# Blocks of 256 queries, values at the end of a pass in a shared bank, and a part of the exponentials on VectorE, in a two-layer transformer on one core

## The chip, the core and the metric

The kernel runs on one core of one Trainium2 chip. A core has TensorE (PE) for matrix products, ScalarE (ACT), VectorE (DVE), GpSimd (POOL) and SyncE (SP), which issues the DMAs here. Each has its own list of instructions, and semaphores make one engine wait for another. PSUM is the memory that TensorE writes to here; the kernel uses eight banks of it, each 512 float32 columns on 128 partitions. The metric is the device time of the whole kernel in microseconds (us).

## The reference

Two layers with the same weights, each an attention and an FFN on x of 2048 x 448 (bfloat16), 16 heads of 28 columns, FFN width 1792:

```python
def _A_ref(x, wqkv, wo):                     # H = 16, Dh = 28
    qkv = (x @ wqkv).reshape(B, S, 3, H, Dh).transpose(2, 0, 3, 1, 4)
    q, k, v = qkv[0], qkv[1], qkv[2]
    p = softmax(einsum("bhqd,bhkd->bhqk", q, k) * Dh ** -0.5)
    o = einsum("bhqk,bhkd->bhqd", p, v)
    return o.transpose(0, 2, 1, 3).reshape(B, S, D) @ wo
def _B_ref(x, w1, b1, w2, b2):
    r = maximum(x @ w1 + b1, 0)
    return (r * r) @ w2 + b2
x = A_x
for _ in range(2):
    x = x + _A_ref(layernorm(x), A_wqkv, A_wo)
    x = x + _B_ref(layernorm(x), B_w1, B_b1, B_w2, B_b2)
```

The softmax needs 16 x 2048 x 2048 exponentials per layer, 134 million in all.

## The kernel before, in words

**A planner orders the work.** The kernel is Python that emits instructions. `Planner.run` holds some generators ("streams"), each with a priority. Each yields one `Op` at a time: the engine, an estimated duration, what it depends on (`deps`), a buffer that it acquires (`acq`, a `Res`) and buffers that it gives back (`rel`). The planner always takes the op that can start first on its own clock, ties by priority, and emits its instructions there. So the order on each engine is fixed when the kernel is built, and the chip only follows it with semaphores. A product of TensorE that would make the scores late is put off (`SLACK`).

**Attention.** Queries are taken in blocks (`blocks`, L164): in layer 0 four of 512 rows, in layer 1 two of 512, two of 256, four of 128. Heads go in four groups `g` of four heads, each head padded to 32 partitions, so that four heads' small products lie beside one another in TensorE's array. A *pass* is one query block, one `g` and a range of key tiles. It is cut into *units* of 512 score columns: one head and one 128-key tile for 512 queries, or two key tiles for 256, four for 128. Three units make a *group*: 2048 units, 683 groups.
- `s_stream` (priority 0, L543): scores of a group, keys as rows and queries as columns, into `sc`, three PSUM banks, two such buffers (`R_sc`).
- `e_stream` (priority 1, L558): one exponential on ScalarE, 128 x 1536 from `sc` to `pt` in SBUF (bfloat16), with the softmax's scale.
- `p_stream` (priority 2, L593): values. As soon as the four heads of a step have their exponentials, four products add into the bank `oT`, which belongs to it alone (`ps_o`). A ones column beside V's 28 columns gives the softmax's sums. At the end of a pass VectorE copies `oT` out (L617), or adds it to an earlier part (L619).
- `norm_stream` (priority 3): three small DMAs on SP spread the sums over partitions, to DRAM and back as a broadcast (L650, L662, L669), with VectorE's reciprocal between (L656), then a product (L679). The last block of a layer does it without DMAs (L635, L641).

**The rest of a layer.** When a block's four groups of heads are normalised, `chain` (priority 4 and on) does the output projection (`wo`, L690 adds to x), layernorm (`bn_stats` L310, a Newton rsqrt of 12 small VectorE instructions L331 to L340, L384), transposes (L359, L369), FFN (L417; ReLU L719 on VectorE, or L717 on ScalarE where no scores are left; square L726), and in layer 0 layernorm and QKV of layer 1 for its rows. `mm_tile` (L399) is the helper of all these products: it has one PSUM bank (`ps_m`, `R_m`), and its VectorE evacuation must be planned before the generator goes on. `first_block` does layernorm and QKV of layer 0, 512 rows at a time.

**Layer boundary.** Layer 1 needs all its keys. Its first passes are cut: block 0 with key tiles 0 to 11, block 1 with the same for two groups of heads (`AHEAD`), then tiles 12 to 15 of these.

**Filler.** `heat` (L763) adds products without use where TensorE's planned load over 2.8 us is under 0.74.

PSUM: six banks for the two `sc`, one for `oT`, one for `mm_tile`.

Of the kernel before, what the change touches and what calls it, by code (L numbers as in the profile page):

```python
# [13 lines left out]
P = 128  # L14
# [4 lines left out]
QB = 512  # L19
EPS = 1e-5  # L20
MAGIC = 0x5F3759DF
WARM = 34
GATE = [None, ('Q', 0, 0, 0), ('Q', 0, 1, 0), ('Q', 0, 3, 0)]
AHEAD = range(2)
SLACK = 0.6
WINDOW = 2.8

# [13 lines left out]
class Op:  # L41
    __slots__ = ("eng", "dur", "fn", "deps", "acq", "rel", "mode", "sets", "start", "end", "res", "turn", "ready", "lat", "need", "got")

    def __init__(self, eng, dur, fn, deps=(), acq=None, rel=None, mode="full", sets=(), lat=0.0, need=1):
        self.eng = eng if isinstance(eng, tuple) else (eng,)
        self.dur, self.fn, self.deps, self.mode, self.lat = dur, fn, deps, mode, lat
        self.rel = rel if isinstance(rel, list) else ([] if rel is None else [rel])
        self.acq = acq if isinstance(acq, tuple) else (() if acq is None else (acq,))
        self.sets = sets if isinstance(sets, list) else ([sets] if sets else [])
        self.start = self.end = self.res = self.turn = None  # L50
        self.need, self.got = need, []
# [5 lines left out]
class Planner:  # L57
# [3 lines left out]
    def __init__(self):  # L61
        self.clock = {"PE": 0.0, "ACT": 0.0, "DVE": 0.0, "POOL": 0.0, "DMA": 0.0, "-": 0.0}
        self.mode = None
        self.tok = {}
        self.streams = []
        self.past = []

    def load(self, span):

        now = self.clock["PE"]  # L70
        return sum(e - max(s, now - span) for s, e in self.past if e > now - span) / span
# [5 lines left out]
    def earliest(self, o):  # L77
        t = 0.0
        for d in o.deps:
            if not isinstance(d, Op):  # L80
                d = self.tok.get(d)
            if d is None or d.end is None:
# [3 lines left out]
                                (0.0 if same and d.eng[0] != "DMA" else LAT[d.eng[0]])))  # L86
        if o.acq:
            free = [r.when() for r in o.acq if r.when() is not None]
# [13 lines left out]
    def run(self):  # L102
        while self.streams:
# [16 lines left out]
            if o.acq:  # L120
                o.res = min((r for r in o.acq if r.when() is not None), key=lambda r: r.when())
# [4 lines left out]
            if e == "PE":  # L126
                self.mode = o.mode
                self.past = [p for p in self.past if p[1] > s - 8.0] + [(s, o.end)]
# [13 lines left out]
def kernel(  # L142
# [19 lines left out]
    scale = float(DH) ** -0.5  # L162

    blocks = [[(0, 4), (4, 4), (8, 4), (12, 4)], [(0, 4), (4, 4), (8, 2), (10, 2), (12, 1), (13, 1), (14, 1), (15, 1)]]  # L164
# [5 lines left out]
    ptp = ctx.enter_context(tc.tile_pool(name="ptp", bufs=4))  # L170
    xtp = ctx.enter_context(tc.tile_pool(name="xtp", bufs=3))
    hp = ctx.enter_context(tc.tile_pool(name="hp", bufs=NFC))
    rp = ctx.enter_context(tc.tile_pool(name="rp", bufs=2))
    np_ = ctx.enter_context(tc.tile_pool(name="np_", bufs=2))
    sp = ctx.enter_context(tc.tile_pool(name="sp", bufs=4))
    dp = ctx.enter_context(tc.tile_pool(name="dp", bufs=2, space=bass.MemoryType.DRAM))
    ps_sc = ctx.enter_context(tc.tile_pool(name="ps_sc", bufs=2, space=bass.MemoryType.PSUM))
    ps_o = ctx.enter_context(tc.tile_pool(name="ps_o", bufs=1, space=bass.MemoryType.PSUM))
    ps_m = ctx.enter_context(tc.tile_pool(name="ps_m", bufs=1, space=bass.MemoryType.PSUM))
# [3 lines left out]
    R_sc, R_o, R_m, R_pt = Res(2), Res(1), Res(1), Res(4)  # L183
    R_xt, R_os, R_xn, R_h, R_on, R_rec = Res(3), Res(2), Res(2), Res(1), Res(2), Res(2)
# [16 lines left out]
    part_sb = const.tile([P, G, QB], DT.float32, name="part_sb")  # L201


    k0_f32 = K_sb[0][:, :, :].rearrange("p g s -> p (g s)").bitcast(DT.float32)
    part = [[part_sb[:, g, :] for g in range(G)], [k0_f32[:, g * QB:(g + 1) * QB] for g in range(G)]]
    st_qk = part_sb[:, :, :].rearrange("p g q -> p (g q)").bitcast(DT.bfloat16)[:, 0:NDC * 2 * D]
# [8 lines left out]
    def setup():  # L215
# [15 lines left out]
        idle = ps_o.tile([P, QB], DT.float32, name="oT")  # L231
# [57 lines left out]
    def bank(o, name):  # L289

        if o.res is R_m:
            return ps_m.tile([P, 512], DT.float32, name=name, tag="m")[:, :]
# [3 lines left out]
    def pools_now(early=False):  # L296
        return (R_m, R_sc) if early or len(s_left) == 0 else (R_m,)

    def engs_now(early=False):
        return ("ACT", "DVE") if (early and ("s", 0) not in pl.tok) or len(s_left) == 0 else ("DVE",)  # L300
# [3 lines left out]
    def moments():  # L304
        return sp.tile([P, 4, 2], DT.float32, name="mv"), []

    def stats(mv, t0, j, deps):
        def fn(e):
            st = sp.tile([P, 6], DT.float32, name="st")
            nc.vector.bn_stats(out=st[:, :], in_=x_sb[:, t0 + j, :])  # L310
# [5 lines left out]
    def layernorm(t0, nt, deps_of, early=False, mv=None):  # L316
# [7 lines left out]
        mv = mv[0]  # L324
        rstd = sp.tile([P, 4], DT.float32, name="rstd")

        def rsqrt(e):
            ve = sp.tile([P, 4], DT.float32, name="ve")
            tt = sp.tile([P, 4], DT.float32, name="tt")
            y, v, t = rstd[:, 0:nt], ve[:, 0:nt], tt[:, 0:nt]  # L330
            nc.vector.tensor_scalar(out=v, in0=mv[:, 0:nt, 1], scalar1=EPS, scalar2=None, op0=ALU.add)  # L331
            yi = y.bitcast(DT.int32)
            nc.vector.tensor_scalar(out=yi, in0=v.bitcast(DT.int32), scalar1=1, scalar2=None,
                                    op0=ALU.arith_shift_right)
            nc.vector.tensor_scalar(out=yi, in0=yi, scalar1=-1.0, scalar2=float(MAGIC),
                                    op0=ALU.mult, op1=ALU.add)
            for _ in range(3):
                nc.vector.scalar_tensor_tensor(out=t, in0=y, scalar=-0.5, in1=y, op0=ALU.mult, op1=ALU.mult)
                nc.vector.tensor_tensor(out=t, in0=t, in1=v, op=ALU.mult)
                nc.vector.scalar_tensor_tensor(out=y, in0=t, scalar=1.5, in1=y, op0=ALU.add, op1=ALU.mult)  # L340
        rs = Op("DVE", 2.3, rsqrt, deps=[last])
# [3 lines left out]
        def take(e):  # L345
            box["x"] = xtp.tile([P, NDC, QB], DT.bfloat16, name="xnT")
# [28 lines left out]
        for p0 in range(0, nt, 2):  # L375
# [4 lines left out]
            for j in js:  # L380
                xn = xns[2 * (own.turn % 2) + j % 2]

                def norm(e, j=j, xn=xn):
                    nc.vector.tensor_scalar(out=xn[:, 0:D], in0=x_sb[:, t0 + j, :],  # L384
                                            scalar1=mv[:, j, 0:1], scalar2=rstd[:, j:j + 1],
# [13 lines left out]
    def mm_tile(subs, evac, ev_dur, deps, any_engine=False, sets=(), early=False):  # L399
# [7 lines left out]
        while i < len(mms):  # L407
# [5 lines left out]
            def fn(e, part=mms[i:k], i=i):  # L413
                if i == 0:
                    box["t"] = bank(first, "mt")
                for c0, n, lhsT, rhs, a, b in part:
                    nc.tensor.matmul(box["t"][:, c0:c0 + n], lhsT=lhsT, rhs=rhs, start=a, stop=b)  # L417
            last = Op("PE", dur, fn, deps=list(deps) if i == 0 else [last],
                      acq=pools_now(early) if i == 0 else None)
# [3 lines left out]
        e = Op(engs_now(early) if any_engine else ("DVE",), ev_dur, lambda e: evac(e, box["t"]), deps=[last], rel=first, sets=sets)  # L423
        yield e
        return e

    def copy_to(dst):
        def f(e, t):
            src = t[:, :] if len(dst.shape) == 2 else t[:, :].rearrange("p (r n) -> p r n", r=dst.shape[1])
            if e == "ACT":  # L430
# [5 lines left out]
    def qkv(l, t0, nt, xnT, own_xt, ends, early=False):  # L436
# [4 lines left out]
        def turned(w, dst, key, wkey, g0):  # L441
# [5 lines left out]
                copy_to(d), 0.70, [*ends, *[(wkey, g) for g in range(g0, g0 + r)]], True,  # L447
# [42 lines left out]
    def first_block(blk):  # L490
        early = blk == 0
        xnT, own_xt, ends = yield from layernorm(4 * blk, 4, lambda j: [("x", blk, j // 2)] + ([] if early else [GATE[blk]]), early)
        yield from qkv(0, 4 * blk, 4, xnT, own_xt, ends, early)
# [9 lines left out]
    add_passes(0, [0], [0, 4, 8, 12, 16])  # L503
    for qb in range(1, len(blocks[0])):
        add_passes(0, [qb], [0, 16])
    add_passes(1, [0], [0, 12])
    add_passes(1, [1], [0, 12], AHEAD)
    add_passes(1, [0], [12, 16])
    add_passes(1, [1], [12, 16], AHEAD)
    add_passes(1, [1], [0, 16], range(AHEAD[-1] + 1, G))  # L510
    for qb in range(2, len(blocks[1])):
        add_passes(1, [qb], [0, 16])
# [8 lines left out]

    def s_stream():
        for gi, us in enumerate(groups):
            deps = set()
            mm = 0
            for pi, kb, r, hh in us:
# [6 lines left out]
            def fn(e, gi=gi, us=us):  # L533
                sc = gbuf[gi]["sc"] = ps_sc.tile([P, 3 * 512], DT.float32, name="sc", tag="sc")
                for i in range(4):
                    for k, (pi, kb, r, hh) in enumerate(us):
                        if i >= r:
# [10 lines left out]
                                   sets=("s", gi))  # L548
# [3 lines left out]
    def e_stream():  # L552
        for gi, us in enumerate(groups):
            n = len(us) * 512

            def fn(e, gi=gi, n=n):
                pt = gbuf[gi]["pt"] = ptp.tile([P, 3 * 512], DT.bfloat16, name="pt")
                nc.scalar.activation(out=pt[:, 0:n], in_=gbuf[gi]["sc"][:, 0:n], func=AF.Exp, scale=scale)  # L558
            o = gbuf[gi]["e"] = Op("ACT", n / 1200 + 0.068, fn, deps=[("s", gi)], acq=R_pt,
                                   rel=gbuf[gi]["s"], sets=("e", gi))  # L560
            yield o

# [3 lines left out]
    def p_stream():  # L566


        where = {}
        for gi, us in enumerate(groups):  # L570
            for k, (pi, kb, r, hh) in enumerate(us):
                where.setdefault((pi, kb), []).append((gi, k, hh))
        steps = list(where.items())
        last_use = {}
        for si, (_, parts) in enumerate(steps):
            for gi, _, _ in parts:
                last_use[gi] = si
        for si, ((pi, kb), parts) in enumerate(steps):
            l, qb, g, kbs, first, last = passes[pi]
            r = 4 // blocks[l][qb][1]  # L580
            n = blocks[l][qb][1] * P
            opens = kb == kbs[0]
            closes = kb + r - 1 == kbs[-1]
            if opens:
                box = {}

            def fn(e, kb=kb, parts=parts, box=box, opens=opens, l=l, g=g, kbs=kbs, r=r, n=n):
                if opens:
                    box["t"] = ps_o.tile([P, QB], DT.float32, name="oT")
                for i in range(r):  # L590
                    for gi, k, hh in parts:
                        c0 = k * 512 + i * n
                        nc.tensor.matmul(box["t"][DHP * hh:DHP * hh + DHP, 0:n],  # L593
                                         lhsT=V_sb[l][:, kb + i, 4 * g + hh, :],
# [214 lines left out]
```

The softmax here doesn't subtract the row's maximum and nothing guards it: scores larger than these inputs give would overflow.

## Time and profile before

| | |
|---|---|
| median of 4 runs | 964.77 us (963.82 to 967.0) |
| the profiled execution | 964.71 us |
| its span, first to last instruction | 962.9 us |
| mean granted TensorE clock | 0.991 |
| ScalarE busy | 929.5 us |
| TensorE busy, weight loads | 855.0 us, 326.2 us |
| VectorE busy | 433.6 us |

The span is what the profile covers; the execution's own time is 1.8 us longer. A line of the groups reads: line of the kernel, engine, operation, out <- in by the program's names, shape, count; after the first bar the busy microseconds and the mean nanoseconds of one; after the second the idle time of the engine just before them and whom it waited for. Busy time counts overlapping instructions once. Means hold their own overlap, so that busy time over count is the price of one in a full engine. In the slices a digit is tenths of a fortieth of the span.

Some lines of the page for orientation: the TensorE clock in the slices, and the DMA queues.

```profile
PEclk9899999999999999999999999999999999999999
...
q1 hardware_dynamic: 24556, 16.02, 5.8%
```

### The profile page before, as it was taken

How to read it: one execution, taken by the hardware profiler on the slowest of the kernel's cores; microseconds unless marked ns; L12 is line 12 of the kernel's file. 1: busy time of each engine (PE TensorE's matmuls, PEld its weight loads, DVE VectorE, ACT ScalarE, POOL GpSimd, SP SyncE). 2: the span in 40 equal slices, each digit the busy share in tenths (PEclk: the TensorE clock that was granted, in tenths of full speed). 3: DMA queues.
4: the chain of work that ended last, by engine and by line, in shares of the span. 5: the costliest groups of instructions: out<-in, count | busy, mean ns of one | idle time of the engine just before them, and what ended most of it. 6: DMA issues, size and time to landing. Idle time of an engine off the chain costs nothing.

```text
span 962.9 us, 19338 instructions
## 1 busy us (share of the span) xinstructions
PE 855.0 (89%) x8267; PEld 326.2 (34%) x8318; DVE 433.6 (45%) x1016; ACT 929.5 (97%) x701; POOL 7.6 (1%) x16
## 2 busy tenths in 40 slices
PE   8888899899888998889888899898899889988987
PEld 3233222233232332322323233323233333555555
DVE  7844334434355243653445433325525533444454
ACT  5899999999999999999999999999999999999992
POOL 3000000000000000000000000000000000000000
PEclk9899999999999999999999999999999999999999
DMA  9000010000000000000000000010000000000000
GB/s 276 2 1 1 1 38 11 12 12 13 13 8 5 12 13 13 1 1 1 1 1 1 1 1 1 9 39 24 12 22 17 13 18 22 17 20 14 22 11 16
DMA packets 24642, 17.25 MB, mean 18 GB/s; under 512 B 11754, under 2 KB 21547, under 8 KB 24556
## 3 DMA queue, kind: packets, MB, share of 16 engines
q1 hardware_dynamic: 24556, 16.02, 5.8%
q8 instruction: 65, 1.06, 0.5%
q14 instruction: 21, 0.17, 0.1%
HBM read 13.73 MB, written 2.06 MB: 16 GB/s over the span
## 4 chain that ended last, share of the span: by engine, by line
ACT 68%; issue 18%; PE 11%; DVE 2%; DMA 0%; ACTq 0%
ACT pt L558 68%; PE mt L417 4%; PE sc L543 3%; PE oT L593 2%; PE sc L417 1%; PE mt L763 1%; DVE r L719 1%; DVE st L310 0%; DMA x_sb<-in_A_x_dram 0%; DVE x_sb L690 0%; DVE rec L641 0%; DVE xnT L369 0%; PE tp L359 0%; PE den L635 0%; DVE xn L384 0%
## 5 line engine op out<-in xcount | busy, mean ns | idle before, releaser
L558 ACT ACTIVATE pt<-sc 128x1536 bf16<-128x1536 f32 (+1 forms) x683 | 918.1, 1726 | 7.9 <-PE sc L543 7.7
L543 PE MATMUL sc<-Q_sb,K_sb 32*128 32x512 bf16 (+2 forms) x3072 | 269.9, 310 | 52.6 <-ACT pt L558 43.7
L593 PE MATMUL oT<-pt,V_sb 128*32 128x512 bf16 (+2 forms) x3072 | 206.3, 316 | 1.0 <-ACT pt L558 0.6
L543 PEld LDWEIGHTS <-K_sb 32*128 32x128 bf16 x3072 | 98.1, 92 | 298.7 <-issue 287.1
L417 PE MATMUL mt<-xnT,w 128*128 128x512 bf16 (+2 forms) x565 | 116.4, 320 | 17.0 <-DVE r L719 10.6
L719 DVE TENSOR_SCALAR r<-mt 128x512 bf16<-128x512 f32 x106 | 72.8, 687 | 126.5 <-PE mt L417 126.4
L417 PE MATMUL mt<-w,h 128*128 128x448 bf16 x434 | 102.9, 355 | 2.5 <-DVE x_sb L690 1.0
L593 PEld LDWEIGHTS <-V_sb 128*32 128x32 bf16 x3072 | 62.5, 94 | 110.5 <-issue 104.3
L690 DVE TENSOR_TENSOR x_sb<-x_sb,mt 128x448 bf16<-128x448 bf16 x62 | 38.5, 621 | 135.0 <-PE mt L417 134.4
L763 PE MATMUL mt<-xn,ident 128*128 128x448 bf16 x204 | 67.6, 354 | 9.9 <-DVE xnT L369 1.5
L417 PEld LDWEIGHTS <-w 128*128 128x128 bf16 x672 | 50.3, 99 | 57.0 <-issue 41.7
L417 PEld LDWEIGHTS <-h 128*128 128x128 bf16 x448 | 35.2, 97 | 45.4 <-issue 23.9
L726 DVE TENSOR_TENSOR h<-r 128x512 bf16<-128x512 bf16 x114 | 47.5, 418 | 5.0 <-ACT r L717 1.8
L417 PE MATMUL mt<-xnT,wq 128*128 128x512 bf16 x115 | 34.5, 380 | 7.2 <-DVE Q_sb L433 4.1
L310 DVE BATCH_NORM_STATS2 st<-x_sb 128x6 f32<-128x448 bf16 x64 | 39.8, 622 | 2.2 <-DMA x_sb<-in_A_x_dram 0.8
L433 DVE CAST Q_sb<-mt 128x512 bf16<-128x512 f32 x30 | 20.7, 689 | 37.2 <-PE mt L417 37.0
L433 DVE CAST K_sb<-mt 128x512 bf16<-128x512 f32 x29 | 20.0, 691 | 37.1 <-PE mt L417 37.1
L459 DVE CAST V_sb<-mt 128x448 bf16<-128x448 f32 x31 | 19.3, 623 | 34.3 <-PE mt L417 34.3
L417 PE MATMUL mt<-xnT,wk 128*128 128x512 bf16 x103 | 31.1, 390 | 3.4 <-DVE K_sb L433 0.9
L417 PE MATMUL mt<-wv,xnT 128*128 128x448 bf16 x124 | 30.9, 370 | 2.5 <-DVE V_sb L459 2.0
L369 DVE COPY xnT<-tp 128x1024 bf16<-128x1024 bf16 (+1 forms) x31 | 20.9, 673 | 26.9 <-PE tp L359 26.8
L417 PE MATMUL mt<-wo,oTn 128*128 128x448 bf16 x124 | 30.0, 354 | 2.5 <-DVE x_sb L690 1.2
(75 smaller groups left out, 329.2 us busy)
## 6 DMA issues: line engine op xcount, KB each, us to landing
rec<-scr SPq DMA_DIRECT2D x20, 256.0 KB
x_sb<-in_A_x_dram SPq DMA_DIRECT2D x8, 224.0 KB
out_dram<-x_sb SPq DMA_DIRECT2D x16, 112.0 KB
w<-in_B_w_dram SPq DMA_DIRECT2D x1, 1568.0 KB
w<-in_B_w_dram SPq DMA_DIRECT2D x1, 1344.0 KB
rec<-scr SPq DMA_DIRECT2D x8, 128.0 KB
rec<-scr SPq DMA_DIRECT2D x12, 64.0 KB
part_sb<-in_A_wqkv_dram SPq DMA_DIRECT2D x1, 672.0 KB
```

What stands on the lines that cost most here:

```text
L310: nc.vector.bn_stats(out=st[:, :], in_=x_sb[:, t0 + j, :])
L369: nc.vector.tensor_copy(out=dst, in_=tp[:, :, 0:w])
L417: nc.tensor.matmul(box["t"][:, c0:c0 + n], lhsT=lhsT, rhs=rhs, start=a, stop=b)
L433: nc.vector.tensor_copy(out=dst, in_=src)
L459: nc.vector.tensor_copy(out=o, in_=i)
L543: nc.tensor.matmul(sc[:, c0:c0 + nt * P], lhsT=K_sb[l][rows, g, (kb + i) * P:(kb + i + 1) * P], rhs=Q_sb[rows, g, t0 * P:(t0 + nt) * P], s ...
L558: nc.scalar.activation(out=pt[:, 0:n], in_=gbuf[gi]["sc"][:, 0:n], func=AF.Exp, scale=scale)
L593: nc.tensor.matmul(box["t"][DHP * hh:DHP * hh + DHP, 0:n], lhsT=V_sb[l][:, kb + i, 4 * g + hh, :], rhs=gbuf[gi]["pt"][:, c0:c0 + n], start ...
L690: nc.vector.tensor_tensor(out=x_sb[:, tb, :], in0=x_sb[:, tb, :], in1=t[:, 0:D], op=ALU.add)
L719: nc.vector.tensor_scalar(out=r[:, 0:w], in0=t[:, 0:w], scalar1=0.0, scalar2=None, op0=ALU.max)
L726: nc.vector.tensor_tensor(out=h[:, 0:w], in0=r[:, 0:w], in1=r[:, 0:w], op=ALU.mult)
L763: nc.tensor.matmul(t[:, 0:D], lhsT=ident[:, :], rhs=xns[0][:, 0:D], start=True, stop=True)
```

## The change

- **Blocks.** Layer 0: eight blocks of 256 queries. Layer 1: six of 256, four of 128. Layernorm and QKV of layer 0 also go by 256 rows (`first_block`, two blocks early). A unit is then two key tiles for 256 queries; there are still 683 groups, and 120 passes. A 512-wide bank of `mm_tile` takes two results of 256 columns.
- **Values at the end of a pass.** `p_stream` waits until the exponential of a group at 3/8 of the pass (`HOLD`) is planned, then takes two steps at a time (`CHUNK`). The bank `oT` of its own is gone: it takes one of two banks `ps_m`, which `mm_tile` and `heat` use as well (`spare` keeps the next one for it near its start). There are 11 `pt` buffers in place of 4.
- **Exponentials on VectorE.** For some groups (`apart`) ScalarE does the first two units only, and VectorE the third, with seven instructions: the scores come scaled by 2^23 log2(e), so that their integer value plus a bias holds 2^x in exponent and mantissa; the mantissa is split off and mended by a polynomial. A group qualifies if it isn't within five groups of its pass's end, if none is under way, and if VectorE's planned load over 12 us is at most 0.9. The buffer `sc` comes free when both engines have read it.
- **Evacuations** of `mm_tile` are streams of their own (priority 3.5), ahead of the chain.
- **Short rsqrt**: two Newton steps with tuned constants, 8 instructions in place of 12.
- Partial sums lie in the other layer's keys, the staged weights in layer 1's values; the scale of the softmax goes into the copy of Q.
- **Layer boundary**: layer 1's blocks 0 to 2, all heads, in key ranges 0 to 7, 8 to 11, 12 to 15 (`CUTS`).

The core of the diff:

```diff
+QR = 256
-AHEAD = range(2)
-SLACK = 0.6
+EARLY = 2
+AHEAD = (range(0, 4), range(0, 4), range(0, 4))
+SLACK = 0.4
...
+LAG = 5
+LEAD = 60
+LAST = 690
+BUSY = 0.9
+SPAN = 12.0
+NPT = 11
...
+HOLD = 3
+CHUNK = 2
+CUTS = (0, 8, 12, 16)
...
-    blocks = [[(0, 4), (4, 4), (8, 4), (12, 4)], [(0, 4), (4, 4), (8, 2), (10, 2), (12, 1), (13, 1), (14, 1), (15, 1)]]
+    blocks = [[(0, 2), (2, 2), (4, 2), (6, 2), (8, 2), (10, 2), (12, 2), (14, 2)], [(0, 2), (2, 2), (4, 2), (6, 2), (8, 2), (10, 2), (12, 1), (13, 1), (14, 1), (15, 1)]]
...
-    ps_o = ctx.enter_context(tc.tile_pool(name="ps_o", bufs=1, space=bass.MemoryType.PSUM))
-    ps_m = ctx.enter_context(tc.tile_pool(name="ps_m", bufs=1, space=bass.MemoryType.PSUM))
+    ps_m = [ctx.enter_context(tc.tile_pool(name=f"ps_m{i}", bufs=1, space=bass.MemoryType.PSUM)) for i in range(2)]
...
-            for _ in range(3):
-                nc.vector.scalar_tensor_tensor(out=t, in0=y, scalar=-0.5, in1=y, op0=ALU.mult, op1=ALU.mult)
...
+            for k, c in ((1.407904506, 1.6819139), (None, 1.5)):
+                nc.vector.tensor_tensor(out=t, in0=y, in1=y, op=ALU.mult)
...
-        yield e
+        pl.spawn(EV, iter([e, *[p(e) for p in post]]))
...
+    def apart(gi):
+        us = groups[gi]
+        if len(us) < 3 or gi < LEAD or gi > LAST or gi + LAG > ends_at[us[-1][0]]:
+            return False
+        if any(end is None for end in aside.values()) or pl.load(SPAN, "DVE") > BUSY:
+            return False
+        aside[gi] = None
+        return True
...
-            n = len(us) * 512
+            yield Op("-", 0.0, None, deps=[("s", gi)])
+            n = (len(us) - (gi in aside)) * 512
...
+    def a_first(gi):
...
+            nc.vector.tensor_scalar(out=box["i"][:, :], in0=gbuf[gi]["sc"][:, 1024:1536], scalar1=EXP_BIAS,
+                                    scalar2=0.0, op0=ALU.add, op1=ALU.max)
+        c = Op("DVE", 0.70, take, acq=R_v, rel=gbuf[gi]["s"], sets=("y", gi))
...
+    def a_rest(gi, c, box):
...
+        def mant(e):
+            nc.vector.tensor_scalar(out=mi[:, :], in0=i, scalar1=0x007FFFFF, scalar2=0x3F800000,
+                                    op0=ALU.bitwise_and, op1=ALU.bitwise_or)
+        def expo(e):
+            nc.vector.tensor_scalar(out=i, in0=i, scalar1=0x7F800000, scalar2=None, op0=ALU.bitwise_and)
+        def step(src, b):
+            def fn(e):
+                nc.vector.scalar_tensor_tensor(out=h[:, :], in0=src, scalar=b, in1=m, op0=ALU.add, op1=ALU.mult)
...
+        for dur, fn in ((0.42, mant), (0.42, expo), (0.68, step(m, b3)), (0.68, step(h[:, :], b2)),
+                        (0.68, step(h[:, :], b1))):
+            o = Op("DVE", dur, fn, deps=[o])
+            yield o
+        o = Op("DVE", 0.68, close, deps=[o], acq=R_pd, rel=c, sets=("x", gi))
+        aside[gi] = gbuf[gi]["x"] = o
```

## The prediction

> **What bounds the kernel now.** I read the page's parts first: busy time, slices, the chain that ended last. The columns of the first three lines are busy microseconds, share of the span and instructions; the slices are fortieths of the span.
>
> ```profile
> span 962.9 us, 19338 instructions
> ...
> PE 855.0 (89%) x8267; PEld 326.2 (34%) x8318; DVE 433.6 (45%) x1016; ACT 929.5 (97%) x701; POOL 7.6 (1%) x16
> ...
> PE   8888899899888998889888899898899889988987
> ...
> DVE  7844334434355243653445433325525533444454
> ACT  5899999999999999999999999999999999999992
> ...
> ACT 68%; issue 18%; PE 11%; DVE 2%; DMA 0%; ACTq 0%
> ```
>
> ScalarE is full from slice 2 to 39, and the chain runs through it. TensorE reads 89%, but not all of that is work. Next, the groups kept apart by shape (busy, mean of one, then idle time ahead):
>
> ```profile
> L558 ACT ACTIVATE pt<-sc 128x1536 bf16<-128x1536 f32 x682 | 917.1, 1727 | 7.9 <-PE sc L543 7.7
> ...
> L719 DVE TENSOR_SCALAR r<-mt 128x512 bf16<-128x512 f32 x104 | 71.9, 692 | 125.1 <-PE mt L417 125.0
> L763 PE MATMUL mt<-xn,ident 128*128 128x448 bf16 x204 | 67.6, 354 | 9.9 <-DVE xnT L369 1.5 <-DVE xn L384 1.2 <-DVE r L719 0.8
> ...
> L384 DVE TENSOR_SCALAR xn<-x_sb,mv,rstd 128x448 bf16<-128x448 bf16 x64 | 22.5, 392 | 4.0 <-PE mt L763 3.3
> ...
> L679 DVE TENSOR_TENSOR oTn<-oT_sb,rec 128x512 bf16<-128x512 f32 x24 | 16.3, 677 | 14.6 <-DMA rec<-scr 14.5
> ...
> L717 ACT ACTIVATE r<-sc 128x512 bf16<-128x512 f32 x4 | 2.4, 597 | 6.5 <-PE sc L417 6.5
> ...
> L717 ACT ACTIVATE r<-sc 128x256 bf16<-128x256 f32 x2 | 0.8, 377 | 0.0
> ```
>
> The exponentials take 918 us in 683 instructions, 1.344 us each, and wait only 7.9 us. (The 1.727 us mean overlaps its neighbours.) TensorE's 67.6 us at L763 are filler. Its real work is 855.0 - 67.6 = 787.4 us, 82% of the span. The timeline gives the ends: first exponential at 14.48 us, last one done at 939.93 us, 23 us of tail.
>
> ```profile
> 14.48 6.82 ACT L558 ACTIVATE pt<-sc 128x1536 bf16<-128x1536 f32 x5 [0.49 <-PE sc L543]
> ...
> 921.41 18.52 ACT L558 ACTIVATE pt<-sc 128x1536 bf16<-128x1536 f32 x14 [0.43 <-PE sc L543]
> ```
>
> So the time is 14.5 us of start, 925.5 us of exponentials with little idle time, 23 us of tail. The profiled execution took 964.71 us, 1.8 us over its span; the median of the runs is 964.77 us, so I work with this execution and need no correction.
>
> **Exponentials moved to VectorE.** This is the only edit that touches the bound. A 1536-wide instruction becomes 1024 wide for each group "set aside". Worth of one: the two ReLU shapes on ScalarE differ by 597 - 377 = 220 ns for 256 elements, so 440 ns for 512. The exponential by itself takes 1.45 us (timeline); (1450 - 597)/1024 x 512 = 427 ns. The only 1024-wide exponential reads 1130 ns against 1727 ns, but both overlap, so 597 ns is an upper end. I take **0.43 us**.
>
> How many? I count from the diff. The 2048 units still make 683 groups. A group may be set aside if its last unit's pass ends five groups later or more, and a whole 256-query pass is 32 units, 10.7 groups, so some six of each pass qualify; 256 groups in all. Only one may be in flight. If one is possible every 4 or 5 groups, the count is 100; every 6, 66; every 7 to 10, 50; every 3, 112. Interval: the chain on VectorE is seven instructions. The first reads PSUM (0.69 us by L719's row), two are one-input integer operations in SBUF (unknown: between 0.39, L384's row, and 0.69; nearest is L384, scaled to 512 columns 0.45), four take two float inputs (0.68 by L679's row; between 0.42, L726's row for bf16, and 0.69). Sum 0.69 + 2 x 0.45 + 4 x 0.68 = 4.3 us, of which 3.6 us lie ahead of the point where the next may be chosen. VectorE's other work takes 45%, and evacuations go ahead of the chain: 3.6/0.55 = 6.5 us, plus half a microsecond from scores to start, 7 us or 5.4 group times of 1.3 us. Between 100 and 66, and 50 where the evacuations crowd: **75**. Gain 75 x 0.43 = **32 us**; by the ends 50 x 0.427 = 21 and 112 x 0.44 = 49.
>
> The Trainium skill speaks against this edit: "ScalarE: Activation LUTs", Rules for kernel authors, has ScalarE as the only option for exp. The diff builds it from integer and float instructions instead; under the rule the gain would be nothing and the forecast some 963 us. "VectorE: DVE Perf Modes", The perf-mode tier table, gives float32 SBUF two elements a cycle for one-input operations and one for two inputs; for the two integer instructions its formula makes an estimate of 0.42 us each, and the chain 4.25 us. No row here shows either.
>
> VectorE must carry it: 75 x 4.3 = 323 us on top of 433.6. The narrower blocks add more, by the rows: 120 evacuations of passes in place of 66 (104 x 0.42 + 16 x 0.29 = 48 for 37 us), products with the reciprocals +4 us, short reciprocals -3 us, and 34 rsqrts of 8 instructions for 20 of 12, at 0.162 us each, 44 for 39 us. Total 433.6 + 323 + 17 = 774 us, 83% of the new span. It fits, but cover is thin.
>
> **Blocks of 256.** TensorE's price by form, busy time over count, for one 512-wide unit: scores 201.6/1536 = 0.131 us at 512, 2 x 33.9/512 = 0.132 at 256; values 0.100 and 2 x 25.7/512 = 0.100; FFN's first product 0.293 at 512, 2 x 15.6/112 = 0.279 at 256. So narrower matmuls cost nothing here; the weight loads, 326 us for 8318, rise by about 3,700 (3,072 for scores and values, the rest for FFN and QKV) x 0.04 = 145 us beside the matmuls, as in the last fifth of the trace, where ScalarE is full with 128-wide blocks. The norm streams send 64 x 3 small DMAs for 40 x 3: 72 more of 0.3 to 0.54 us on SP, 40 us on a queue that has nothing else from 20 us until the stores. Hidden.
>
> At the layer boundary the work that covers the last chain stays the same length: 288 units, 96 groups, stand before the first keys of tiles 12 to 15, as now (192 + 96 units). Now that stretch holds filler (7.5 us at 600 to 640, 9.9 us at 640 to 680 us), so the chain ends early; if it came late, ScalarE would stand still for as long. Partial sums kept in the other layer's keys, weights staged in layer 1's values and the scale folded into Q's copy change no instruction count and no shape on a full engine: nothing.
>
> **Values at the end of a pass, a shared bank.** The same matmuls, later; ScalarE doesn't wait for them while it has 11 output buffers. TensorE's waits for evacuations are L719 11.0, Q 4.4, x 2.5, V 2.4, K 2.3 us, 23 us together: with a second bank some vanish, but TensorE is not the bound, so I count nothing. The unknown: the wait of a score for its buffer, which a set-aside group gives back only when VectorE has read its third. VectorE's instruction in front (0 to 0.7 us) and the read (0.69) end about when the 1024-wide exponential does. From 0 to 0.7 us each, 0 to 52 us; a score is issued one exponential (1.3 us) ahead, so I take the low end, and **3 us** for all new stalls together.
>
> **Short rsqrt, start and tail.** From the timeline, steps of it follow at 0.195 us. Four fewer are 0.8 us, once on the tail's path (947.04 to 949.32 us). At the start, two tiles of statistics in place of four save 1.4 us, rsqrt 0.8, but the weights' copies on ScalarE end at 11.65 us and K's product now needs the third of them: first exponential some 0.7 us sooner. The second group then needs block 1's keys; the old gap of 4.5 us at 21.3 us may shrink or grow, plus or minus 3 us.
>
> **Sum.** 962.9 - 32.3 - 0.7 - 0.8 + 3 = 932.1, plus 1.8 outside the span: **934 us**.
>
> **Rivals.**
> - *TensorE binds in places* (0.18). For: in the stages without filler, 40 to 120 us, it has 34.6 us of work in 40 us, and about 2.7 us of idle time that is not waiting for exponentials ((963 - 855 - 44)/24): 37.3 in 40, room for 7%, and a value pass holds one of the two banks for most of its length. Against: the set-aside groups speed ScalarE by only 4 to 6% locally. Price: half the gain, 934 + 16 = 950 us.
> - *It doesn't do what it says* (0.10): the gate stays shut since VectorE's load in 12 us passes 0.9. One in flight is 4.3 us, 36%, beside 45 to 50% of other work; two in a window reach 1.2. At 35 groups the gain is 15 us: 951 us.
> - *Slower: VectorE's queue becomes the bound* (0.20). Its instructions come in the planned order; each of about 400 evacuations of TensorE's results can meet a 0.68 us step ahead of it, a mean of 0.34 us. At full price that is 136 us, and TensorE's slack is 963 - 787 - 64 = 112 us, of which the faster exponentials eat 32. It decides once evacuations wait over 0.2 us on the average: 136 - 80 = 56 us beyond the slack, 934 + 56 = 990 us at the worst; middle 975. For: VectorE at 83%, every evacuation feeding one in-order queue. Against: evacuations are written ahead of chain steps, and VectorE now idles 125 us at L719 alone, waiting for TensorE.
>
> **How the numbers follow.** My forecast has 0.52, its own range 915 (112 groups) to 948 (50 groups, 3 us worse start). The rivals have 0.18, 0.10 and 0.20. The range is 908 to 968: the low end adds the start's 3 us and no stalls to 112 groups, the high end takes a part of the slower rival. Measurement tells about 0.2% from no change: faster 0.79, same 0.02 (the edge of the last rival), slower 0.19.
>
> **What would show it.** Right: 683 exponentials, about 75 of them 1024 wide; ScalarE still full; VectorE at 80 to 85%, its chain's first step 0.69 us; scores waiting as little as now; less filler at the junk line; first exponential before 14 us. Wrong: ScalarE idle behind scores that wait for TensorE (second line: first rival) or evacuations that lag TensorE by more than 0.2 us (third); fewer than 50 narrow exponentials (too few groups); over 110 (the interval was shorter than worked out); a hole at the layer boundary, where layer 1's keys come too late.

## The result and the profile after

The changed kernel takes 967.77 us (median of 45 runs, 962.2 to 970.62) against 966.6 us of the kernel before (69 runs): ratio 1.0016, interval 1.0009 to 1.0024. The forecast was 934 us. The gain of 32 us that the set-aside groups were to bring isn't there. The profiled execution took 968.89 us, 1.8 us over its span.

The page of the changed kernel, the same parts as before:

```profile
span 967.1 us, 27524 instructions
...
PE 847.1 (88%) x12074; PEld 429.1 (44%) x12074; DVE 648.3 (67%) x1556; ACT 912.4 (94%) x701; POOL 7.6 (1%) x16
...
PE   8999878988897888888998899779888898888886
...
DVE  7855257677667677677786664147877677686764
ACT  6999999999999999989999899999999999999992
...
ACT 45%; PE 28%; issue 18%; DVE 8%; DMA 0%; ACTq 0%
```

ScalarE has 17 us less work and yet the span is longer: its row now has eights, and the chain that ended last runs 45% through it, down from 68%; TensorE and VectorE took over. So ScalarE waits. For what, the groups kept apart by shape say (idle time ahead and its cause behind the second bar):

```profile
L633 ACT ACTIVATE pt<-sc 128x1536 bf16<-128x1536 f32 x624 | 847.8, 1547 | 13.5 <-PE sc L614 13.0
...
L633 ACT ACTIVATE pt<-sc 128x1024 bf16<-128x1024 f32 x59 | 61.0, 1034 | 13.2 <-DVE vi L645 12.2
...
L645 DVE TENSOR_SCALAR vi<-sc 128x512 int32<-128x512 f32 x58 | 40.0, 689 | 47.7 <-PE sc L614 41.8 <-ACT pt L633 5.6
```

Two waits are there that the kernel before doesn't have. The narrow exponentials wait for VectorE's first instruction of the chain (L645), which computes nothing that they read; and L645 itself stands 41.8 us waiting for scores.

**The ledger.** An idle line undercounts, since an exponential that starts late also loses its overlap with the one before. I therefore take each exponential's end minus the end of the one before: in a full engine 1.343 us for a wide one, 0.916 us for a narrow one (the medians of the wide ones and the shortest narrow ones in the trace, a difference of 0.427 us). What is above that is stall; 2.3 us of it after the change are copies of K, Q and V that ScalarE does between the first exponentials.

| us, profiled executions | before | after |
|---|---|---|
| narrow exponentials | 1 | 59 |
| saved by 58 more narrow ones | | -24.8 |
| stall at wide ones | 8.5 | 19.4 |
| stall at narrow ones | 0 | 18.2 |
| first exponential starts later by | | 0.6 |
| tail after the last exponential | 23.0 | 22.2 |

-24.8 + 10.9 + 18.2 + 0.6 - 0.8 = 4.1 us, and the spans differ by 4.2. The gain was made in full and given back as stalls.

**What a narrow exponential waits for.** The timeline of the changed kernel, start and duration first:

```profile
178.13 0.39 PE L614 MATMUL sc<-Q_sb,K_sb 32*128 32x256 bf16 x6
178.24 0.62 DVE L833 TENSOR_TENSOR x_sb<-x_sb,mt 128x448 bf16<-128x448 bf16 x1 [4.31 <-PE mt L467]
178.78 0.68 DVE L645 TENSOR_SCALAR vi<-sc 128x512 int32<-128x512 f32 x1
...
179.55 1.02 ACT L633 ACTIVATE pt<-sc 128x1024 bf16<-128x1024 f32 x1 [0.47 <-DVE vi L645]
```

Its scores end at 178.52. VectorE first does an evacuation (L833), which itself came 4.31 us after the instruction before it, and then L645. ScalarE is idle for 0.47 us and starts when L645 has ended (178.78 + 0.68 = 179.46), 93 ns later. 51 of the 58 start like this after L645, 49 of them 92 to 94 ns after its end and two 33 ns; in the other seven L645 waits for the exponential. In the built program the instruction waits on VectorE's semaphore. Both read the same buffer `sc`, but other banks of it, and the layer that sets the semaphores puts two readers of a buffer on different engines one after the other. The planner knows nothing of that.

**What TensorE waits for.** The worst place, 406 to 415 us, the lines that carry it:

```profile
406.82 0.39 PE L614 MATMUL sc<-Q_sb,K_sb 32*128 32x256 bf16 x6
...
407.26 0.69 DVE L645 TENSOR_SCALAR vi<-sc 128x512 int32<-128x512 f32 x1 [4.42 <-PE sc L614]
407.54 0.35 PE L467 MATMUL mt<-b2w,one 128*128 128x448 bf16 x1
407.99 0.43 DVE L659 TENSOR_SCALAR vm<-vi 128x512 int32<-128x512 int32 x1
...
408.45 0.43 DVE L663 TENSOR_SCALAR vi<-vi 128x512 int32<-128x512 int32 x1
408.80 0.69 DVE L667 SCALAR_TENSOR_TENSOR vh<-vm 128x512 f32<-128x512 f32 x1
409.51 1.42 DVE L667 SCALAR_TENSOR_TENSOR vh<-vh,vm 128x512 f32<-128x512 f32 x2
410.97 0.69 DVE L672 SCALAR_TENSOR_TENSOR pd<-vh,vi 128x512 bf16<-128x512 f32 x1
411.58 0.61 DVE L833 TENSOR_TENSOR x_sb<-x_sb,mt 128x448 bf16<-128x448 bf16 x1
...
412.25 0.54 PE L909 MATMUL mt<-xn,ident 128*128 128x448 bf16 x2 [3.22 <-DVE x_sb L833]
412.71 0.40 PE L614 MATMUL sc<-Q_sb,K_sb 32*128 32x256 bf16 x6
...
413.30 0.68 DVE L645 TENSOR_SCALAR vi<-sc 128x512 int32<-128x512 f32 x1
...
414.01 0.61 PE L614 MATMUL sc<-Q_sb,K_sb 32*128 32x256 bf16 x6
414.07 2.37 ACT L633 ACTIVATE pt<-sc 128x1024 bf16<-128x1024 f32 x2 [3.66 <-DVE vi L645]
```

VectorE stands 4.42 us at L645, whose scores come at 407.2. The FFN's last product ends at 407.89, but its evacuation L833 is behind the whole chain and starts at 411.58, 3.7 us late. TensorE's next instruction is filler (L909) that needs that bank: 3.22 us. The next scores stand behind the filler, and ScalarE loses 3.66 us. The ledger has this at a narrow exponential, but only some 0.9 us of it, from the scores' end at 413.11 us on, are the wait for L645. Then the clock follows: from 413.0 to 423.3 us the windows give a granted clock of 0.50, and six score products take 0.61 us in place of 0.40. In all, TensorE runs 44 us at half clock, before the change 18 us; these sums, here and below, run to the end of the clock's record, up to 2 us after the last instruction.

Why was the chain ahead of the evacuation? In `a_first` the op of L645 has `acq=R_v` and no `deps` on its scores. The stream does wait for them with an empty op, but that sets no lower bound on the next op's start, so the planner puts L645 and the chain where its VectorE is free, in some places before the scores exist. By the planner's own clock that is so for 24 of the 58 chains, by up to 4.0 us.

### The profile page after: what moved, and what is told of

Same layout as the page of the kernel before. It is cut to its first block, busy times and chain, and to the rows that moved or that the text cites. A ratio compares the mean times of both kernels' runs of the same rounds, so it can differ in the third digit from the quotient of the medians.

```text
span 967.1 us, 27524 instructions
## 1 busy us (share of the span) xinstructions
PE 847.1 (88%) x12074; PEld 429.1 (44%) x12074; DVE 648.3 (67%) x1556; ACT 912.4 (94%) x701; POOL 7.6 (1%) x16
## 4 chain that ended last, share of the span: by engine, by line
ACT 45%; PE 28%; issue 18%; DVE 8%; DMA 0%; ACTq 0%
ACT pt L633 45%; PE mt L467 11%; PE sc L614 7%; PE oT L736 5%; PE mt L909 2%; DVE vi L645 2%; DVE vh L667 2%; PE sc L467 1%; DVE vm L659 1%; DVE x_sb L833 1%; DVE vi L663 0%; DVE r L864 0%; PE tp L409 0%; DVE st L357 0%; DVE pd L672 0%
## 5 line engine op out<-in xcount | busy, mean ns | idle before, releaser
L633 ACT ACTIVATE pt<-sc 128x1536 bf16<-128x1536 f32 (+1 forms) x683 | 900.9, 1503 | 26.8 <-PE sc L614 13.0
L614 PE MATMUL sc<-Q_sb,K_sb 32*128 32x256 bf16 (+1 forms) x4608 | 273.9, 262 | 84.1 <-ACT pt L633 76.8
L736 PE MATMUL oT<-pt,V_sb 128*32 128x256 bf16 (+1 forms) x4474 | 160.3, 267 | 1.0 <-DVE x_sb L833 0.4
L467 PE MATMUL mt<-xnT,w 128*128 128x256 bf16 (+1 forms) x952 | 124.9, 268 | 6.7 <-DVE r L864 4.0
L467 PEld LDWEIGHTS <-w 128*128 128x128 bf16 x1008 | 82.0, 100 | 45.7 <-issue 36.2
L909 PE MATMUL mt<-xn,ident 128*128 128x448 bf16 x296 | 93.9, 370 | 9.6 <-DVE x_sb L833 5.0
L667 DVE SCALAR_TENSOR_TENSOR vh<-vh,vm 128x512 f32<-128x512 f32 x116 | 79.5, 685 | 1.2
L645 DVE TENSOR_SCALAR vi<-sc 128x512 int32<-128x512 f32 x58 | 40.0, 689 | 47.7 <-PE sc L614 41.8
L833 DVE TENSOR_TENSOR x_sb<-x_sb,mt 128x448 bf16<-128x448 bf16 x62 | 38.3, 617 | 43.4 <-PE mt L467 42.9
L672 DVE SCALAR_TENSOR_TENSOR pd<-vh,vi 128x512 bf16<-128x512 f32 x58 | 39.7, 685 | 1.2 <-PE mt L467 0.5
L667 DVE SCALAR_TENSOR_TENSOR vh<-vm 128x512 f32<-128x512 f32 x58 | 39.5, 681 | 0.0
L909 PEld LDWEIGHTS <-ident 128*128 128x128 bf16 x296 | 22.1, 97 | 38.3 <-issue 33.9
L467 PE MATMUL mt<-xnT,wk 128*128 128x256 bf16 x256 | 35.5, 274 | 2.3 <-DVE xnT L419 1.7
L467 PE MATMUL mt<-xnT,wq 128*128 128x256 bf16 x240 | 33.6, 274 | 0.2
```

The lines of the kernel that those rows point to most:

```text
L467: nc.tensor.matmul(box["t"][:, c0:c0 + n], lhsT=lhsT() if callable(lhsT) else lhsT, rhs=rhs, start=a, stop=b)
L614: nc.tensor.matmul(sc[:, c0:c0 + nt * P], lhsT=K_sb[l][rows, g, (kb + i) * P:(kb + i + 1) * P], rhs=Q_sb[rows, g, t0 * P:(t0 + nt) * P], s ...
L645: nc.vector.tensor_scalar(out=box["i"][:, :], in0=gbuf[gi]["sc"][:, 1024:1536], scalar1=EXP_BIAS, scalar2=0.0, op0=ALU.add, op1=ALU.max)
L667: nc.vector.scalar_tensor_tensor(out=h[:, :], in0=src, scalar=b, in1=m, op0=ALU.add, op1=ALU.mult)
L672: nc.vector.scalar_tensor_tensor(out=pd[:, :], in0=h[:, :], scalar=b0, in1=i.bitcast(DT.float32), op0=ALU.add, op1=ALU.mult)
L736: nc.tensor.matmul(box["t"][DHP * hh:DHP * hh + DHP, 0:n], lhsT=V_sb[l][:, kb + i, 4 * g + hh, :], rhs=p[:, c0:c0 + n], start=begin and kb ...
```

## The experiments

Theories: **A**, the wait between the two readers of a buffer; **B**, the chain planned before its scores, with evacuations, TensorE and its clock behind it; **C**, VectorE simply has too much work; and a rival that the blocks or the shared bank cost the time. "Stall" is that of the ledger, from the profiled execution, whose own time is given; ratios are to the kernel before on the same chip.

**A alone: the readers free of each other.** Nothing of the order changes, only the wait between the two goes; the scores that reuse the buffer now wait for both.

```diff
-                nc.scalar.activation(out=pt[:, 0:n], in_=gbuf[gi]["sc"][:, 0:n], func=AF.Exp,
+                ex = gbuf[gi]["ei"] = nc.scalar.activation(out=pt[:, 0:n], in_=gbuf[gi]["sc"][:, 0:n], func=AF.Exp,
...
+                if "ti" in gbuf[gi]:
+                    tc.declare_no_dep(ex.ins, gbuf[gi]["ti"].ins, reason="two readers of two banks")
...
+            ex = gbuf[gi].get("ei")
+            if ex is not None:
+                tc.declare_no_dep(tk.ins, ex.ins, reason="two readers of two banks")
+            gbuf[gi]["ti"] = tk
```

> The changed kernel, but the narrow exponential on ScalarE and the first instruction of the chain on VectorE, which read different banks of one score buffer, no longer wait for each other. In the changed kernel's trace 51 of 58 narrow exponentials start 93 ns after that VectorE instruction ends, and 18 us of stall stand at them. Theory A (this wait is what ate the gain): 968.9 - 16 = 953 us, stalls at the narrow ones under 3 us, those at wide ones unchanged (19 us). Theory B (the chain is put into VectorE's queue before its scores exist, and evacuations behind it come late): the stall moves from the narrow exponential to the next score, which needs the buffer back; at most 6 us gained, 963 us or more. Theory C (VectorE simply has too much work): no change, 967 to 969 us.

Measured 956.75 us, ratio 0.9882 (0.9846 to 0.9918): 11 us of the 16. In the profiled execution, the slowest of its four (963.31 us), the stall at narrow ones fell from 18.2 to 5.5 us, that at wide ones rose from 19.4 to 27.2 us, with TensorE 54 us at half clock. A is real, though neither theory's numbers were met: 5.5 us are left at the narrow ones for under 3, and the wide ones weren't unchanged. Whether part of the stall moves on to the next scores, as B had it, isn't shown: the rise at the wide ones fits it, but this execution is 6.6 us slower than the median.

**B alone: the chain planned after its scores.**

```diff
-        c = Op("DVE", 0.70, take, acq=R_v, rel=gbuf[gi]["s"], sets=("y", gi))
+        c = Op("DVE", 0.70, take, deps=[("s", gi)], acq=R_v, rel=gbuf[gi]["s"], sets=("y", gi))
```

> The changed kernel with one dependency more in the plan: the first instruction of a chain is planned only after its scores (the plan lacked it, and put it up to some microseconds too early). 51 groups are set aside in place of 58, worth 3 us. Theory B: VectorE's wait for scores at the chain's first instruction falls from 42 us to a few, the stalls at wide exponentials from 19 to about 9 us, those at narrow ones from 18 to some 10 us (0.2 us each, the wait between the two readers stays), TensorE's time at half clock from 44 us to about 20: 968.9 - 18 + 3 = 954 us. Theory A: stalls at narrow ones stay near 15 us, at wide ones near 19: 969 us. Theory C: 967 to 972 us.

Measured 957.26 us, 0.9904 (0.9872 to 0.9936). Stall at wide ones 11.2 us, at narrow ones 9.6, half clock 30 us (profiled execution 955.52 us): near what B said (9, 10, 20 us and 954). Evacuations of the adds to x start more than 1 us after their product's end 3 times, in the changed kernel 8 times, in the kernel before never. One expectation failed: L645 still waits 35 us for scores. That idle time costs nothing by itself; the harm was in what stood behind it.

**Both.** The two edits together.

> Both edits: planned after the scores, and the two readers free of each other. If A and B are both at work: stalls at narrow ones 1 us, at wide ones 9 us: 968.9 - 27 + 3 = 945 us. If only A: 956 us, like the first of these kernels with 7 groups fewer. If only B: 953 us. Theory C: 967 to 972 us.

Measured **945.76 us**, 0.9783 (0.9758 to 0.9808). Stall at narrow ones 0.0, at wide ones 11.1 us. The groups of this kernel, where no narrow exponential waits any more:

```profile
L633 ACT ACTIVATE pt<-sc 128x1536 bf16<-128x1536 f32 x631 | 861.6, 1661 | 6.5 <-PE sc L614 6.3
...
L633 ACT ACTIVATE pt<-sc 128x1024 bf16<-128x1024 f32 x52 | 64.1, 1233 | 0.0
...
L647 DVE TENSOR_SCALAR vi<-sc 128x512 int32<-128x512 f32 x51 | 35.0, 686 | 34.7 <-PE sc L614 34.5
```

The gains add: 11.0 and 10.5 us singly against 967.77, 22.0 together. C falls: VectorE is busy 66% here, 67% in the changed kernel, and 76% in the fastest version below.

**No group set aside** (`LAST = -1`).

> The changed kernel with no group set aside: all exponentials on ScalarE, the blocks, the shared bank and the rest as in the change. Theories A and B: the exponentials cost 58 x 0.427 = 25 us more and the stalls fall from 38 to about 9 us: 968.9 + 25 - 29 = 965 us, that is, the rest of the change is worth nothing and the set-aside groups paid for themselves alone. A rival, that the blocks and the shared bank cost the time: stalls stay at 25 us or more, 980 us.

Measured 960.76 us, 0.9934 (0.9908 to 0.996). Stall 4.7 us in all, less than before the change (8.5). So the rest of the change is worth some 6 us (in the profiled executions 3.8 of stalls, 2.9 of them in the first 50 us, and 1.5 of tail), and the rival falls. As built the set-aside groups cost 7 us in place of saving 25; with both edits they save 15 of the 22 that 51 groups are worth.

**More groups, with both edits** (`LAG = 3`, then `LAG = 2`).

> Both edits, and a group may be set aside up to three groups before its pass's end (five so far): 69 groups in place of 51. Each is worth 0.427 us as long as the stalls stay at 11 us: 945.8 - 7.7 = 938 us. Rival (VectorE's work begins to cost: it goes from 66% to some 71%): evacuations wait, stalls at wide exponentials rise to 18 us or more, 945 us or more.

> Both edits, up to two groups before the pass's end: 75 groups. At constant stalls 945.8 - 10.3 = 935.5 us; by the rival, 945 us or more, with stalls at 20 us, since the value products of a pass's last steps now wait for chains that end with it.

Three: 946.23 us, 0.9787 (0.9753 to 0.982), no gain. Two: **936.3 us, 0.9695 (0.966 to 0.973)**, 3% under both kernels. With three, the last exponential ends 3 us sooner than with five, but the tail is 26.8 us in place of 22.0, 10 us of it with TensorE at half clock, and stalls are 15.8 us. With two, stalls are 16.3 us, the tail 22.8. VectorE is busy 73% and 76%. So 18 and 24 groups more brought 0 and 9.5 us, of 7.7 and 10.3 at constant stalls. With three, the added stalls and the longer tail make up the difference. With two the forecast was met within 1 us, though the profiled execution, 4 us slower than the median, has the larger stalls; VectorE's load alone thus doesn't decide, and why three is worse than two stays open.

**The clock and the filler.** In the profiled version with two (940.34 us), larger stalls lie at or within 3 us after stretches at half clock (12 of the 13 over 0.4 us after the first 50 us):

```profile
302.32 0.61 PE L614 MATMUL sc<-Q_sb,K_sb 32*128 32x256 bf16 x6
...
302.87 1.89 PE L467 MATMUL mt<-xnT,w 128*128 128x256 bf16 x8
...
304.68 0.61 PE L614 MATMUL sc<-Q_sb,K_sb 32*128 32x256 bf16 x6
...
305.40 1.45 ACT L633 ACTIVATE pt<-sc 128x1536 bf16<-128x1536 f32 x1 [0.91 <-PE sc L614]
...
307.51 0.39 PE L614 MATMUL sc<-Q_sb,K_sb 32*128 32x256 bf16 x6
```

Eight FFN products take 1.89 us at half clock, so the scores behind them are too late for ScalarE. Two kernels change the filler's threshold, the second takes the filler out:

```diff
-            short = 0.74 - pl.load(WINDOW)
+            short = 0.82 - pl.load(WINDOW)
...
-            short = 0.74 - pl.load(WINDOW)
+            short = -1.0
```

> The last version with 75 groups, filler where TensorE's planned load is under 0.82 in place of 0.74. That version still stalls 16 us, and its TensorE runs 44 us at half clock; each of the larger stalls lies in or right after such a stretch. Theory D (idle TensorE halves the clock, and the products then make the scores late): half clock falls to some 25 us, stalls to 11 us, 931 us. Rival (filler stands in front of real work): stalls stay or rise, 936 to 946 us.

> The same version without any filler, 73 groups. Theory D: half clock above 100 us, stalls at 30 us or more, 950 us or more. Rival (filler is only in the way): 930 to 936 us.

More filler: 943.05 us, 0.9778 (0.9757 to 0.9799): half clock down from 44 to 33 us, but stalls up from 16.3 to 18.3 us. Of these, 8.2 us are a single wait, at the layer boundary:

```profile
593.86 0.70 DVE L434 TENSOR_SCALAR xn<-x_sb,mv,rstd 128x448 bf16<-128x448 bf16 x2
...
597.70 0.69 DVE L488 CAST K_sb<-mt 128x512 bf16<-128x512 f32 x1 [1.96 <-PE mt L467]
...
599.62 2.79 ACT L633 ACTIVATE pt<-sc 128x1536 bf16<-128x1536 f32 x2 [8.14 <-PE sc L614]
```

The scores wait there for layer 1's last keys, which L488 starts to copy out at 597.70 us; in the version with two this copy starts at 583.19 us, without filler at 577.91 us. All other stalls together fell to some 10 us, close to the 11 of theory D. So away from this place D holds; at it the rival fits, since the keys come later the more filler is planned, but that the filler itself delays them isn't shown. The medians, 6.8 us apart, differ by more than the profiled executions, 1.9 us.

None: 952.99 us, 0.9872 (0.9855 to 0.9889), half clock 186 us, stalls 26.3 us. The clock row of its page and that of the version with two and the old filler:

```profile
PEclk9999658999897989989999998568999998889998
```

```profile
PEclk9999999999998999999989999999999999999999
```

So the clock matters (17 us between no filler and the old threshold, two groups fewer aside), and filler has its own price. How the 16 us that are left divide between the two stays open.

## Why the prediction was wrong, point by point

- **The bound**: right. ScalarE's exponentials set the time before, and what moved the time after was their stalls.
- **Price of a set-aside group**: right, 0.427 us measured, 0.43 said. **Count**: 58 for 75, above my lower end of 50; 24.8 us for 32.3. None lies before 133 us, and none starts between 566 and 658 us, around the layer boundary.
- **VectorE's chain**: 0.69 + 2 x 0.42 + 0.68 + 3 x 0.685 = 4.27 us for 4.3. Its load came out at 67% for 83%: fewer groups, and neighbours overlap (its instructions' durations sum to 712 us, 648 us without the overlap).
- **The step that failed**: "3 us for all new stalls together". Measured 10.9 + 18.2 = 29 us, and against the kernel with no group set aside 37.6 - 4.7 = 33 us. With the 7.5 us of missing groups and the 1.3 us at the start, the 26 us too few here make up the 35 us between the forecast's span and the measured one. Two waits were missing, A and B; freed singly they gave back 11.0 and 10.5 us. I bounded the wait of a score for its buffer at 0 to 0.7 us per group and took the low end, since it and the read "end about when the 1024-wide exponential does". I never asked whether the exponential itself waits for that read: I took two readers of one buffer as free of each other. The stall has a mean of 0.31 us at the narrow exponentials (18.2/58), some 0.2 us of it from this wait (9.6/51 with the order mended; (18.2 - 5.5)/58 by taking the wait away). That the total lies within the 0 to 52 us that I had worked out and left out of the sum is chance: those were for another wait.
- **The rival "VectorE's queue becomes the bound"** named the right place: evacuations behind chain steps, TensorE behind them, deciding "once evacuations wait over 0.2 us on the average". The adds to x wait 0.37 us on the average, 0.05 before. But its cause was wrong, and so was my argument against it. Not the load: with 76% busy and a right order they wait 0.16 us; the 83% of the forecast was never reached. And "evacuations are written ahead of chain steps" holds only for ops that the planner sees at their true time; L645 had no dependence on its scores, which could be read in the diff (`Op("DVE", 0.70, take, acq=R_v, ...)`).
- **"It doesn't do what it says"** didn't come: 58 groups were set aside, not its 35. The saving was made and given back.
- **Blocks of 256**: right. A unit of scores costs 2 x 239.5/3584 = 0.134 us of TensorE for 0.132 said, weight loads rose by 103 us for 145. **Values in one burst** were better than said: they take 160 us of TensorE, 206 before.
- **The rest of the change** is worth some 6 us, as the kernel with no group set aside shows; the sum had 0.7 + 0.8 = 1.5 us for it.
- **Filler**: wrong way. 296 products in place of 204; TensorE's own work fell, so there is more to fill.
- **Start**: off by 1.3 us in the profiled execution, where the first exponential comes 0.6 us later, not 0.7 sooner. That is within its scatter: in the nine profiled kernels with this start it comes at 14.34 to 15.28 us, before the change at 14.48. The old gap of 4.6 us became three of 1.0 to 1.3 us. **Tail**: -0.8 us as said, in part by luck: with no group set aside it is -1.5 us.
- **The range**: its low end doesn't come out of its own terms; 112 groups, no stalls and 3 us at the start make 962.9 - 49.3 - 0.7 - 0.8 - 3 + 1.8 = 910.9 us, not 908.

## What to carry to other kernels

Before work is moved to a second engine that reads the same buffer, look in the built program at which semaphores the two readers wait on: a layer that tracks buffers may order them though neither writes. In a kernel whose order is planned on paper, an op without its data dependence isn't wrong on the chip, only late, and everything behind it in that engine's queue is late with it; so check each new op for its dependences in the plan, not only in the data. And sum an engine's end-to-end intervals, not its idle lines: here the lines showed 27 us of 38.

## What the runs showed of the hardware

- Idle time on TensorE can cost a second time. Stretches at a granted clock of 0.50 last 3.4 us or a multiple, begin a multiple of 3.41 us apart within a run, and each begins right after 3.41 us in which TensorE was idle for a good part: in the changed kernel for 1.19 to 3.02 us of them (2.65 us before the stretch at 413.01, 2.21 us before that at 529.06), in the version with `LAG` of two for 1.04 to 2.12 us. So idle time of some 1.0 to 1.2 us within such a window came before a halved clock. It doesn't decide alone: in the changed kernel 1.34 us from 300.4 to 303.8 us wasn't followed by one. The Trainium skill, "TensorE: Matmul & The Clock Gate", HAM oscillation, says that gaps of over about 3.4 us throttle the array; the length of the window agrees with these stretches, the threshold doesn't.
- ScalarE and VectorE read different banks of one PSUM buffer at once without loss: with both edits, where the two overlap in time in 49 of 51 groups, the first chain step takes 686 ns (689 in the changed kernel), and narrow exponentials end 0.917 us after their predecessors (median; the shortest of the changed kernel 0.916). The Trainium skill, "PSUM — Partial Sum Buffer", Specifications (TRN2), says that the two read in parallel at full rate as long as they don't meet in a bank; these numbers agree.
- Values taken in bursts of two steps cost TensorE 46 us less (160 for 206) than one step at a time, in more and narrower instructions. Width isn't the reason: 256-wide ones took 50 ns each before (25.7/512) and take 37 ns with no group set aside (133.4/3584). That the bursts are is likely but not shown, since no run takes single steps.
